# Block-causal attention with a ReGLU network: the last quarter of the result by row blocks on two queues, and another order of tiles 3 to 8

## The chip, the cores and the metric

The kernel runs on one core of a Trainium2 chip. The core has five engines, each of which carries out its own instructions in the order of the program: PE (matmuls; its weight loads, PEld, run beside the products), DVE (VectorE), ACT (ScalarE), POOL (GpSimd) and SP (SyncE, which here only issues transfers). An engine waits on semaphores for what another engine or a transfer has to deliver. The metric is the device time of one execution in microseconds; lower is better.

## The reference

```python
# 8 batches, 8 heads, 576 positions, head dim 64; blocks of 64 positions
scores = scale * np.matmul(q, k.transpose(0, 1, 3, 2))      # scale = 1/8
scores = np.where(block_i >= block_j, scores, -1e9)         # causal by blocks
attn = softmax(scores)
x = np.matmul(attn, v)  # -> [batch, position, head, dim] -> [4608, 512]
gate = np.maximum(x @ w_gate, 0.0)                          # w_gate [512, 1536]
val = x @ w_val                                             # w_val  [512, 1536]
out = (gate * val) @ w_out                                  # w_out [1536, 512]; out [4608, 512], fp32
```

## The kernel before

**Tiles.** The network is worked off in nine tiles of 512 rows. Tiles 0 to 7 are the first 512 positions of batches 0 to 7, and tile 8 is the last 64 positions of all eight batches. Attention runs ahead of the network: tiles 0 to 2 and the attention of batches 0 to 3 come in a hand-written order of their own (ORDER_0), and in each of tiles 3 to 6 the attention of the next batch, and the loads of the batch after that, are woven into the network's products. Tiles 7 and 8 have no attention beside them.

**The order.** Nothing is scheduled by a compiler: `program(j)` returns a function `do`, and a string of words (ORDER_3_6 for tiles 3 to 6, ORDER_7, ORDER_8) is read word by word; `w*n` repeats a word n times. Each word emits one step, and so the string sets the order of instructions on all engines at once. The words:

- `g8`, `v8`: a quarter (an atom) of a plain product with w_gate or w_val for 128 of the 1536 columns; four make one bank of 512 columns. `r8` is its relu on ACT, `h8` the multiply on DVE.
- `p37`: an atom of product 7 of pair 3. Pairs of column blocks (six pairs, 0 to 5) are done by a scheme of seven products in place of eight, so with sums of parts of x and of the weights as operands; each of the seven products has two atoms, each of two matmuls of 256 columns. `p3a`, `p3u`, `p3w` are ACT's copies of a bank to SBUF, `p3d`, `p3e`, `p3c` DVE's adds of a bank to such a copy, `p3r` a relu on ACT. `p3H` and `p3L` multiply gate by value into the two halves of hT, the low half always on DVE (line 1395), the high half on DVE or GpSimd (line 1391).
- `M1` to `M7`: an atom of one of the seven output products (line 1060), which read hT or sums of it. Six atoms make a whole product: three for the rows p = 0 and then three for p = 1.
- `oa`, `ou`, `ow`, `oy`: ACT copies a bank of the result to SBUF (line 1105); `od`, `oe`, `oc`: DVE adds a bank to such a copy (line 1099). The result has four quarters, c11, c12, c21 and c22; c12 is the bank `w` as it stands once M1, M6, M5 and M3 have been summed in it, c21 an earlier copy of `w` to which the bank of M7 and M4 is added.
- `S0` to `S2`: the store of a quarter by `put_block`; `P` is the store S3 of the tile before. In tiles 3 to 7 a store is one issue, by ACT (line 892). In tile 8 it is two issues (line 905), one for each half of the partitions, since its rows belong to eight batches; a table there gives the issuing engine by quarter.
- `X4` to `X7`, `Y4` to `Y7`: sums of parts of x (line 1161). `s1302`: part 3 of the sums of hT for the pairs 2 and 3 (line 1019). `U45`: a sum of weights, redone in each tile because its memory is shared.
- `A0` to `A3`: the score products of two heads of the next batch; `E0u`, `E0s` and so on the exps that follow on ACT (line 635); `C01` the zeroing of a corner of the exps; `V01` the products with v (line 778); `N01` the normalising on DVE.
- `l0` to `l10`, `w0` to `w5`: loads of q, k and of v in bf16 for the batch after next, issued by GpSimd (line 508). `d0` to `d3`: the transposes of q and k (qTm, kTm, qTt, kTt) by DMA, on SyncE's queue (line 518). `T0` to `T3`: the transposes of x into xT, also on SyncE's queue.

**Who does what.** The set ON_POOL names the steps that GpSimd does in place of DVE, with the tile ahead (`3X5`, `8s1202`). SLOTS, PAIR_BANK, OUT_BANK and AV_BANK name the buffer or PSUM bank of each step; there are two banks of a kind `sc`, one `one` and three `ffn`.

**The end of the program.** The last words of ORDER_8 are `M3*4 Sa M3*2 oy S0 oe S1`: the last product, a copy of all of c12 by ACT, its store, which the table gives to SyncE twice (`(0, 256)`), the add of c21 on DVE, and its store, which the table gives to ACT twice (`(1, 0)`). The words stand in each engine's program in this order, and each engine reaches its own as soon as what it needs is there.

Of the kernel before, what the change touches and what calls it, by code (L numbers as in the profile page):

```python
# [17 lines left out]
def kernel(  # L18
# [91 lines left out]
    ORDER_8 = """  # L110
        X4 p01 p17 p07 p21 p01 p07 p11*2 p17 p12 p21 p12 p0a p06 p1a p1c p06 p16*2 p0w
        p04*2 p0u p05 p0e p05 p0d p1u p15*2 p1w p14 p1d p14 p1e p1L p31*2 p02*2 p0c p03
        p2a p3a p03 p0r p0H p13*2 p1r p1H p26*2 p2u p27*2 p0L p41*2 p32*2 p3c p25 p36
        p2w p25 p36 p2d p24*2 p2e p4a p3u p37 p22*2 p2c p37 p23*2 p3w p2r p51*2 s0002
        p2L p35*2 p3d p42 P p5a p34*2 p3e p3L p42 p47*2 p4w p33*2 p56 p46 p3r s0202
        s0102 p4c p46 p4u p44 p52*2 p5c p56 p44 p4e p57*2 p2H p45*2 p4d p5u p55*2 p5w
        p5d M7 p54*2 p5e M1 p43 M1 p53*2 M2*2 p5r p4L p43 p4r p5L M1*4 oa p5H p4H s2002
        s2202 M2*4 p3H s1002 s1102 s2302 s2102 s1202 M6*5 M7 M6 ou s0302 ocb Sb oca M7*4
        M5*5 ow M4 M5 M4*3 od S2 M4*2 s1302 M3*4 Sa M3*2 oy S0 oe S1
# [40 lines left out]
        (7, 4): ('sc', 'ffn', 'one'),  # L160
        (7, 5): ('sc', 'ffn', 'ffn'),
        (8, 0): ('sc', 'one', 'one'),
        (8, 1): ('ffn', 'ffn', 'ffn'),
        (8, 2): ('sc', 'ffn', 'one'),
        (8, 3): ('ffn', 'ffn', 'one'),
        (8, 4): ('sc', 'sc', 'one'),
        (8, 5): ('ffn', 'ffn', 'ffn'),
# [1639 lines left out]
```

## Time and profile before

| | us |
|---|---|
| three runs | 346.49, 347.24, 347.37 |
| their median | 347.24 |
| the profiled execution's own time | 348.3 |
| its span, first to last instruction | 346.5 |
| busy in the span: PE / DVE / ACT / POOL | 333.9 / 239.8 / 211.2 / 202.4 |
| mean granted clock of PE | 0.998 |

The profile comes from one execution, with instruction times on each engine; the span is shorter than the execution's time by what lies ahead of the first and behind the last instruction. A row of the sums by stage gives a stretch of the span and the busy time of each engine in it. A row of the chain gives the start and length of a stretch of the work that ended last, its engine and line. A row of the waits reads: who waited, for which engine's line, the sum of the waits, their number, and the longest. An engine name with a q behind it (ACTq, SPq) is the engine's sequencer: there an issue of a transfer shows as the time that the engine was taken up with it.

### The profile page before, as it was taken

The numbers are of one execution on the slowest core, as the hardware profiler recorded it, in microseconds if no ns is written. First come the engines' busy times: TensorE is split into PE (matmuls) and PEld (weight loads), VectorE is DVE, ScalarE is ACT, GpSimd is POOL, SyncE is SP. The second block draws the span as 40 slices with busy tenths as digits, with TensorE's granted clock in tenths as the row PEclk, the third lists the DMA queues.
The fourth block names the chain that finished last, engine by engine and source line by source line (L and its number), as shares of the span: only waits on it lengthen the run. The fifth ranks groups of instructions, "written<-read, shape, count | busy, mean of one in ns | idle before, by whom it ended". The sixth has DMA issues, their size and how long they took to land.

```text
span 346.5 us, 8901 instructions
## 1 busy us (share of the span) xinstructions
PE 333.9 (96%) x3477; PEld 234.0 (68%) x3518; DVE 239.8 (69%) x561; ACT 211.2 (61%) x348; POOL 202.4 (58%) x249
## 2 busy tenths in 40 slices
PE   8999999999999999999999999999999999999993
PEld 4544455545545559676867787778777798878883
DVE  4854445768628887588638874788478877995991
ACT  4942757587325872787467865876487717626740
POOL 2766565588965902846866758675514673820720
PEclk9999999999999999999999999999999999999999
DMA  8999999999998994999399999999510030002004
GB/s 237 294 352 373 363 235 243 230 149 185 171 231 93 140 176 95 203 137 144 61 167 146 116 97 153 150 116 112 132 47 2 19 99 32 2 30 93 32 1 121
DMA packets 155402, 50.06 MB, mean 144 GB/s; under 512 B 134464, under 2 KB 151744, under 8 KB 155360
## 3 DMA queue, kind: packets, MB, share of 16 engines
q0 software_dynamic: 70528, 8.98, 44.5%
q1 hardware_dynamic: 77520, 32.52, 43.4%
q10 hardware_dynamic: 7312, 8.00, 8.0%
q8 instruction: 27, 0.44, 0.5%
q14 instruction: 15, 0.12, 0.1%
HBM read 37.75 MB, written 9.44 MB: 136 GB/s over the span
## 4 chain that ended last, share of the span: by engine, by line
PE 84%; ACT 4%; DVE 3%; DMA 3%; ACTq 2%; issue 2%; SPq 0%; POOL 0%; DVEq 0%
PE ffnp L1169 15%; PE ffnp L1353 10%; PE sc L1353 8%; PE one L1060 7%; PE ffnp L1329 6%; PE ffnp L1060 6%; PE ffnp L1272 6%; PE one L1353 5%; PE sc L1060 4%; PE sc L630 3%; PE ffnp L778 2%; PE one L630 2%; DMA stage<-in_moe_w_val_dram 2%; ACTq L892 2%; PE sc L778 2%
## 5 line engine op out<-in xcount | busy, mean ns | idle before, releaser
L635 ACT ACTIVATE attnT<-sc 128x1024 bf16<-128x1024 f32 x56 | 56.2, 1035 | 0.0
L1179 ACT ACTIVATE gate_sb<-ffnp 128x512 bf16<-128x512 f32 x35 | 20.5, 598 | 27.2 <-PE ffnp L1169 24.3
L1169 PE MATMUL ffnp<-xT,wg 128*128 128x512 bf16 x130 | 36.2, 379 | 0.6
L1060 PEld LDWEIGHTS <-stage 128*128 128x128 bf16 x336 | 31.9, 98 | 4.5 <-DVE stage L1019 0.5
L1353 PEld LDWEIGHTS <-stage 128*128 128x128 bf16 x288 | 27.6, 98 | 7.6 <-issue 0.7
L778 PEld LDWEIGHTS <-attnT 128*128 128x128 bf16 x640 | 26.8, 98 | 8.2 <-DVE xnat L717 1.2
L1169 PE MATMUL ffnp<-xT,wv 128*128 128x512 bf16 x108 | 31.3, 380 | 0.2
L1189 DVE TENSOR_TENSOR hT<-gate_sb,ffnp 128x512 bf16<-128x512 bf16 x28 | 19.2, 684 | 14.3 <-PE ffnp L1169 11.5
L1353 PEld LDWEIGHTS <-wg 128*128 128x128 bf16 x224 | 21.5, 98 | 7.9 <-issue 3.0
L1060 PEld LDWEIGHTS <-hT 128*128 128x128 bf16 x252 | 23.7, 98 | 4.0 <-DVE hT L1395 1.3
L1379 DVE TENSOR_TENSOR ob<-ffnp,ob 128x512 f32<-128x512 f32 x29 | 19.9, 688 | 8.9 <-ACT ob L1375 6.6
L508 POOL DMA_DIRECT2D v_bf<-in_v_dram x30 | 24.5, 838 | 2.7 <-PE ffnp L1169 1.1
L1353 PEld LDWEIGHTS <-wv 128*128 128x128 bf16 x224 | 21.4, 98 | 5.1
L1272 PE MATMUL ffnp<-wo,hT 128*128 128x512 bf16 x91 | 23.1, 379 | 0.2
L1169 PEld LDWEIGHTS <-wg 128*128 128x128 bf16 x144 | 13.4, 98 | 13.8 <-issue 0.5
L1169 PEld LDWEIGHTS <-wv 128*128 128x128 bf16 x144 | 13.0, 98 | 14.3 <-issue 1.5
L508 POOL DMA_DIRECT2D q_bf<-in_q_dram x20 | 18.1, 910 | 6.3 <-DVE recip L751 6.2
L1324 ACT ACTIVATE gate_sb<-ffnp 128x512 bf16<-128x512 f32 x29 | 17.8, 612 | 6.4 <-PE ffnp L1353 4.8
L642 ACT ACTIVATE attnT<-one 128x512 bf16<-128x512 f32 (+1 forms) x28 | 15.2, 543 | 10.5 <-PE ffnp L630 10.4
L1391 POOL TENSOR_TENSOR hT<-gate_sb,q_bf 128x512 bf16<-128x512 bf16 x8 | 10.2, 1285 | 19.4 <-ACT gate_sb L1324 19.3
L1105 ACT COPY ob<-one 128x512 f32<-128x512 f32 x13 | 7.6, 586 | 22.0 <-PE one L1060 22.0
L630 PEld LDWEIGHTS <-kTm 64*128 64x128 bf16 x384 | 11.4, 94 | 13.1 <-issue 7.0
(223 smaller groups left out, 919.3 us busy)
## 6 DMA issues: line engine op xcount, KB each, us to landing
out_dram<-ob ACTq DMA_DIRECT2D x28, 256.0 KB, 3.2
stage<-in_moe_w_val_dram SPq DMA_DIRECT2D x6, 512.0 KB, 8.7
stage<-in_moe_w_gate_dram SPq DMA_DIRECT2D x6, 512.0 KB, 8.3
stage<-in_moe_w_out_dram SPq DMA_DIRECT2D x6, 512.0 KB, 10.5
q_bf<-in_q_dram POOLq DMA_DIRECT2D x20, 128.0 KB, 5.4
k_bf<-in_k_dram POOLq DMA_DIRECT2D x20, 128.0 KB, 5.7
v_bf<-in_v_dram POOLq DMA_DIRECT2D x20, 128.0 KB, 6.7
stage<-in_v_dram SPq DMA_DIRECT2D x19, 128.0 KB, 5.4
```

Source lines behind the costliest of these rows:

```text
L508: ins = nc.gpsimd.dma_start(dst, part_of)
L630: nc.tensor.matmul(o, kTm[b % 2][head_of(hh), c, hp, :], qT, start=True, stop=True)
L635: return lambda: nc.scalar.activation(at[:, :, lo : lo + 512], sc, AF.Exp, scale=scale)
L778: nc.tensor.matmul(av[:, p, :], at[:, col : col + 128], v_bf[b % 2][:, c, h, :], start=(p == 0), stop=(c == p), skip_group_check=True,)
L1060: nc.tensor.matmul(to, sums.of(c)[which][:, 128 * p : 128 * p + 128], right, start=first, stop=(c == 5), skip_group_check=True,)
L1169: nc.tensor.matmul(to, (wg, wv)[t][f // 4][:, c, 128 * (f % 4) : 128 * (f % 4) + 128], x[:, c], start=(c == 0), stop=(c == 3),)
L1179: nc.scalar.activation(gate_sb, gate, AF.Relu)
L1189: nc.vector.tensor_tensor(out=h, in0=gate_sb, in1=val, op=AX.mult)
L1272: nc.tensor.matmul(op, hT[f][:, 128 * s : 128 * (s + 1)], wo[f // 4][:, f % 4, n0:n1], start=(f == 0), stop=(f == 11),)
L1329: nc.tensor.matmul(to, (wg, wv)[t][f // 4][:, c, 128 * (f % 4) : 128 * (f % 4) + 128], x[:, c], start=(c == 0), stop=(c == 3),)
L1353: nc.tensor.matmul(st[key][:, 256 * k : 256 * k + 256], left[:, c, 128 * k : 128 * k + 128], right[:, c], start=new and (k, c) == (0, 0), ...
L1379: nc.vector.tensor_tensor(out=t, in0=st[n, of], in1=t, op=AX.add)
```

## The change

The last quarter of tile 8's result, c12, is no longer copied by ACT in one piece and stored by SyncE in two issues. The new steps `oya` and `oyb` copy the rows p = 0 (ACT, behind the third atom of M3) and the rows p = 1 (DVE, behind the sixth), and `Sya` and `Syb` store each with two issues of half the size, one by SyncE and one by ACT. The store of c21 goes from ACT and ACT to GpSimd and SyncE.

Beside this the strings for tiles 3 to 8 are replaced by others with the same products, copies, adds and stores. What differs most: the transposes `d0` to `d3` stand earlier than `T0`, with `d1` to `d3` ahead of all of `T0` to `T3`; S2 is stored behind `od` instead of at the end of the tile; the numbers of M2 and M3 behind M4 change; and the order of pairs in tiles 7 and 8 is another. ON_POOL changes: in tiles 3 to 6 the multiply 5H goes from GpSimd to DVE, X4, X5 and X7 are on GpSimd in place of X5 and X6, the sums of hT there are s0002, s1002, s1102 and s2302 in place of five others, and of the corners C01, C10, C20, C21, C30, C31 in place of C01, C11, C20, C21, C31. U03 is on GpSimd and U46 is not. In tile 8 seven sums of hT are on GpSimd in place of three. SLOTS, PAIR_BANK, OUT_BANK and AV_BANK follow the new order and are left out below.

```diff
--- before.py
+++ after.py
...
@@ -83,40 +83,40 @@
         x15 f*2 U57 f*20
     """.split()
     ORDER_3_6 = """
-        X5 A0 E0u E0s E0f g0*2 p12 g1 p12 g1 l0 X7 X6 X4 l1 l2 l3 p11*2 p1a g0*2 C00 p1c
-        E0t r0 g1 p17*2 p16 g1 K k p16 C01 V00 N00 v1*2 p1u p15*2 p1w p1d V01 N01 p14*2
-        p1e p1L v1 p13*2 v0*2 A1 P v1 r1 h1 p1r v0 p21 E1t E1u v0 h0 E1s p21 p2a p22*2
-        p2c p31 E1f p27 g8*2 p27 p2w p26*2 p2u U45 p1H s0002 p37 p31 p3a C10 p24*2 p2e
-        p32 p25*2 p2d l4 l5 l6 w0 l7 l8 s0202 C11 p2L w1 g8 p36*2 p3u V11 N11 p37 p3w g8
-        r8 p35*2 p3d p23*2 p2r p34*2 p3e p32 p33*2 p3r p3c A2 E2t p51*2 v8*2 p57*2 E2u
-        p52*2 p2H l9 l10 s0102 p3L p5a w2 w3 p3H s1002 p5c v8 p56 v8 h8 p56 p5w E2s C21
-        p54*2 U05 p5u p5e g9 E2f g9*3 r9 V10 N10 p55*2 p5d p5L v9*2 A3 E3t E3u v9*2 h9
-        d0 d1 T0 T1 d2 p53*2 p5r C20 U46 V20 M1 p5H s1102 N20 s2102 s2002 s1202 s2202
-        E3f V21 M1*3 M7*2 M1*2 E3s C30 M7*2 C31 N21 d3 T2 w4 s1302 s2302 U07 w5 oa M7*2
-        ow M6*2 V30 N30 M6*4 V31 N31 T3 M4*2 ou M5*6 U06 od M4*4 oe S1 M2 U03 s0302 M3*6
-        oy S0 U47 U43 M2*5 S2 oc
+        A0 l0 X5 w0 g1*3 E0t X7 X6 E0s g0*4 E0u C01 E0f C00 p11 K p11 p12 p1a p12 p1c l1
+        k g1 r1 p17*2 w1 p16*2 p1u V00 N00 v1*2 p15*2 p1w p1d P r0 X4 l2 l3 d0 V01 N01
+        v1 p14*2 p13*2 p1r p1e v0*2 v1 A1 E1t E1s v0*2 p1H h1 h0 p1L p21*2 p2a p22*2 p2c
+        p27*2 p2w p26 U05 p26 p2u U06 l4 l5 l6 p31*2 p3a p24*2 p2e w2 s0002 p25*2 p2d
+        U45 g8 E1f E1u C11 g8*2 p36*2 p2L p37 p3u p37 p3w w3 C10 V11 p23 N11 p23 p2r
+        p35*2 p3d g8 r8 p34*2 p3e p32*2 p3c s0102 p33*2 U46 l7 l8 l9 p3L d1 l10 d2 d3 w4
+        w5 p3r p3H A2 E2u E2t p51*2 p5a p2H s1002 E2s C21 v8*2 p52*2 s1102 p5c p57 v8
+        p57 p5w v8 h8 p56*2 p5u V10 N10 T1 T0 g9 p54*2 p5e g9*3 p55*2 p5d E2f r9 U43 A3
+        E3u v9*2 p53*2 v9 s1202 C20 M1*2 p5L M1*2 M7 v9 s0202 U07 s0302 M1*2 V21 M7 E3f
+        p5r E3s p5H C30 h9 s2002 s2102 s2202 E3t C31 V20 s2302 V31 oa M6*4 V30 M6*2 N21
+        N20 T2 M7*4 ou N30 N31 M5*3 M2 M5*3 ow od S2 U03 M4*3 T3 M2 M4 s1302 U47 M3 M4*2
+        oe S1 M2 M3*5 oy S0 M2*3 oc
     """
     ORDER_7 = """
-        X5 p11*2 p1a p01*2 p0a X7 X6 p21 p02 p12*2 p1c X4 p07*2 p16 p02 p06 p0c p16 p06
-        p0w p04*2 p21 p22 p0u p0e p1u p05*2 p0d p22 p15 p17 p0L p2a p2c p17 p15 p1w p1d
-        p03*2 p26 p0r p0H p31*2 p14 p27 p3a p27 p14 p1e p13 p37 p13 p1r p1H s0002 p1L
-        s0102 p36 p26 p36 p32*2 p3c Y5 p51*2 p37 p2u p25 p2w p25 p2d p24*2 p2e p5a p56
-        p3u p35*2 p23 p41 p23 p41 p3w p3d p2r p2H p34*2 p57 p33*2 p57 p56 p2L p4a p46
-        p3e p3L p52*2 p3r p5u p5w p42 p5c p42 p4c p3H p55*2 p5d p46 p47 p54 p47 p4u p54
-        p5e p4w p45*2 p4d M2 p44*2 p4e p53*2 M1*2 p5L p4L p5r p43 M2 p43 p4r p5H s0202
-        p4H s2002 M1*2 M7 s1002 s1202 M1*2 M2*3 s2202 s1102 M7 M2 oa M6*6 s2102 M7*4 P
-        ou M5*6 s2302 Y7 s0302 s1302 ow od S2 M4*5 oc M4 oe M3*6 oy S1 S0 Y6
+        p11*2 p12 p01*2 p21 p02 p12 Y5 X5 X7 X6 X4 p1a p1c p0a p02 p0c p07 p06*2 p0u p07
+        p0w p16 p17 p16 P p1u p05 p17 p05 p0d p04*2 p0e p21 p15*2 p1w p2a p03 p22 p03
+        p14*2 p0r p0H p1d p13*2 p1r p22 p26*2 p31 p2u p0L p2c p1e p1H p31 p3a p37*2
+        p27*2 p2w p1L s0002 s0202 p25 p32 p25 p2d p36*2 p3u p24*2 p2e p32 p3w p23*2 p2r
+        p2H p51 p3c p35*2 p3d p34*2 p3e p51 p5a p41*2 p4a p33*2 p3r p3H p56*2 p5u s1002
+        p2L p46 p52*2 p57*2 p5w p46 p4u p3L s1102 p5c s0102 p55*2 p5d p47 p42*2 p4c p47
+        p54 p4w p54 p5e p45*2 p4d p44*2 p4e p5L p4L M1 M2 p53 p43 M1 p53 p5r p5H M7*2
+        p43 M2 p4r p4H s2002 s2202 s2102 s1202 M1*4 M2*4 oa M6*6 ou s1302 M7*4 M5*6 ow
+        od S2 M4*6 s0302 M3 s2302 Y7 M3*5 oe S1 oy S0 Y6 oc
     """
     ORDER_8 = """
-        X4 p01 p17 p07 p21 p01 p07 p11*2 p17 p12 p21 p12 p0a p06 p1a p1c p06 p16*2 p0w
-        p04*2 p0u p05 p0e p05 p0d p1u p15*2 p1w p14 p1d p14 p1e p1L p31*2 p02*2 p0c p03
-        p2a p3a p03 p0r p0H p13*2 p1r p1H p26*2 p2u p27*2 p0L p41*2 p32*2 p3c p25 p36
-        p2w p25 p36 p2d p24*2 p2e p4a p3u p37 p22*2 p2c p37 p23*2 p3w p2r p51*2 s0002
-        p2L p35*2 p3d p42 P p5a p34*2 p3e p3L p42 p47*2 p4w p33*2 p56 p46 p3r s0202
-        s0102 p4c p46 p4u p44 p52*2 p5c p56 p44 p4e p57*2 p2H p45*2 p4d p5u p55*2 p5w
-        p5d M7 p54*2 p5e M1 p43 M1 p53*2 M2*2 p5r p4L p43 p4r p5L M1*4 oa p5H p4H s2002
-        s2202 M2*4 p3H s1002 s1102 s2302 s2102 s1202 M6*5 M7 M6 ou s0302 ocb Sb oca M7*4
-        M5*5 ow M4 M5 M4*3 od S2 M4*2 s1302 M3*4 Sa M3*2 oy S0 oe S1
+        p07 X4 p07 p01*2 p0a p17 p11*2 p12 p1a p12 p1c p06*2 p31 p0w p0u p16*2 p1u p04*2
+        p0e p17 p1w p05*2 p0d p15*2 p1d p14*2 p1e p1L p31 p3a p03*2 p0r p37 p13*2 p1r
+        p1H p21 p0H s0002 p21 p02*2 p0c p0L s0102 p36 p27*2 p2a p26*2 p32 p37 p32 p3c
+        p41*2 p2u p25*2 p36 P p2w p2d p24*2 p3w p2e p4a p34*2 p3u p3e p23*2 p2r p2H
+        p22*2 p2c p35*2 p3d p51 p47 p51 p5a p42 p47 p4w p46 p52 p42 p3L p46 p4c p2L p44
+        p33*2 p4u p44 p4e p3r p45*2 p4d s0202 p4L p52 p56*2 p5c M2 p57*2 p5u p55 p43 p55
+        p5w p5d M2 p43 p4r p54*2 p5e p5L p4H M1 p53 M7 p53 p5r M1*4 M2 p3H M1 M2*3 p5H
+        s2002 s1102 M7 s1002 s1202 s2202 s2302 s1302 s2102 oa oca M6 s0302 M6*5 ou Sa
+        M7*4 M5*6 ow od S2 ocb Sb M4*4 M3*3 oya Sya M4*2 oe S1 M3*3 oyb Syb
     """
     ONLY = {
         'U03': (6,),
...
     ON_POOL = set(
         """
-        32H 35H 3C01 3C11 3C20 3C21 3C31 3X5 3X6 3s0202 3s0302 3s1002 3s1302
-        3s2302 42H 45H 4C01 4C11 4C20 4C21 4C31 4X5 4X6 4s0202 4s0302 4s1002
-        4s1302 4s2302 52H 55H 5C01 5C11 5C20 5C21 5C31 5X5 5X6 5s0202 5s0302
-        5s1002 5s1302 5s2302 62H 65H 6C01 6C11 6C20 6C21 6C31 6X5 6X6 6s0202
-        6s0302 6s1002 6s1302 6s2302 70H 71H 72H 73H 7X4 7X5 7s0002 7s0102 7s0302
-        7s1002 7s1102 7s2302 80H 81H 82H 83H 8s0102 8s1002 8s1202 U05 U06 U43
-        U45 U46
+        32H 3C01 3C10 3C20 3C21 3C30 3C31 3X4 3X5 3X7 3s0002 3s1002 3s1102
+        3s2302 42H 4C01 4C10 4C20 4C21 4C30 4C31 4X4 4X5 4X7 4s0002 4s1002
+        4s1102 4s2302 52H 5C01 5C10 5C20 5C21 5C30 5C31 5X4 5X5 5X7 5s0002
+        5s1002 5s1102 5s2302 62H 6C01 6C10 6C20 6C21 6C30 6C31 6X4 6X5 6X7
+        6s0002 6s1002 6s1102 6s2302 70H 71H 72H 73H 7X4 7X5 7X7 7Y6 7s0002
+        7s0202 7s1002 7s1102 7s1202 7s2302 81H 82H 83H 8s0002 8s0102 8s0202
+        8s1002 8s1102 8s1302 8s2302 U03 U05 U06 U43 U45
         """.split()
     )
...
@@ -898,8 +898,8 @@
             for i in range(2):
                 b0 = 4 * hi + 2 * p0 + i
                 eng = {
-                    (0, 256): (nc.sync, nc.sync),
-                    (1, 0): (nc.scalar, nc.scalar),
+                    (0, 256): (nc.sync, nc.scalar),
+                    (1, 0): (nc.gpsimd, nc.sync),
                     (1, 256): (nc.sync, nc.gpsimd),
                 }.get((hi, n0), (nc.scalar, nc.sync))
                 eng[i].dma_start(
@@ -1109,6 +1109,15 @@
                 add(st["c21"], st["v"])
             elif name == "oc":
                 add(st["c11"], st["x"])
+            elif name in ("oya", "oyb"):
+                if "c12" not in st:
+                    st["c12"] = ob()
+                p = "ab".index(name[2])
+                copy = (nc.scalar.copy, nc.vector.tensor_copy)[p]
+                copy(half(st["c12"], p), half(st["w"], p))
+            elif name in ("Sya", "Syb"):
+                p = "ab".index(name[2])
+                put_block(j, 0, 256, half(st["c12"], p), p, p + 1)
             elif name in ("oca", "ocb"):
                 p = "ab".index(name[2])
                 add(half(st["c11"], p), st["x", p])
...
```

More of the change, by code (lines that the diff above doesn't have):

```diff
@@ L45 @@
         "sc": (
-            "010101010101010010101010101010101010101010101010101010101001100100110101"
-            "10011001001101011001100100110101100110010011010110001010101"
+            "010101010101010010101010101010101010101010101010101010101001011100111010"
+            "01101000110001011001011100111010011010001100010110010110101100"
         ),
@@ L50 @@
             "021021021020210210210210210210120210120202010101210120201201120120210211"
-            "201021102101020120120120121201202101202101202101210201021201021001001201"
-            "201020121020120020021021020102120102100100120120102012102012002002102100"
-            "0201210210021210102"
+            "201021102101020120120120121201202101202101202101210221012021210220201212"
+            "012201021202012212102021022101202121022020121201220102120201221210202100"
+            "20012120102202210"
         ),
         "ob": (
-            "043210432104314013240312402312301243021340231230124302134023123012430213"
-            "402312302130214201240312"
+            "043210432104314024130413023413240213241320341304201304130234132402132413"
+            "203413042310423402431024"
         ),
         "gate_sb": (
-            "021021021021021021021021021021021021021201012010212102120101201021210210"
-            "21021021"
+            "021021021021021021021021021021021021021102210122011202110221012201120210"
+            "21021201"
         ),
@@ L155 @@
         (6, 5): ('ffn', 'one', 'ffn'),
-        (7, 0): ('ffn', 'one', 'sc'),
-        (7, 1): ('sc', 'sc', 'ffn'),
+        (7, 0): ('ffn', 'one', 'ffn'),
+        (7, 1): ('sc', 'sc', 'sc'),
         (7, 2): ('ffn', 'ffn', 'ffn'),
         (7, 3): ('one', 'ffn', 'sc'),
[L160 to L167, printed above, removed]
+        (7, 4): ('ffn', 'ffn', 'one'),
+        (7, 5): ('sc', 'ffn', 'sc'),
+        (8, 0): ('one', 'sc', 'sc'),
+        (8, 1): ('ffn', 'sc', 'ffn'),
+        (8, 2): ('sc', 'one', 'ffn'),
+        (8, 3): ('ffn', 'ffn', 'ffn'),
+        (8, 4): ('sc', 'one', 'ffn'),
+        (8, 5): ('ffn', 'one', 'sc'),
     }
@@ L188 @@
     }
-    AV_BANK = {0: ('ffn', 'one'), 1: ('sc', 'sc'), 2: ('ffn', 'ffn'), 3: ('ffn', 'sc')}
+    AV_BANK = {0: ('one', 'ffn'), 1: ('sc', 'sc'), 2: ('sc', 'ffn'), 3: ('one', 'ffn')}
     LAST_CHUNKS = {}
```

2 lines of the change are left out of this document (1 added, 1 removed).

## The prediction

> **What bounds the kernel now.** I read the page's head first, then the sums by stage, the chain that ended last, the waits of TensorE, and last the order of time around three places: the starts of tiles, the start of each tile's output products, and the tail.
>
> ```profile
> span 346.5 us, 8901 instructions
> ...
> PE 333.9 (96%) x3477; PEld 234.0 (68%) x3518; DVE 239.8 (69%) x561; ACT 211.2 (61%) x348; POOL 202.4 (58%) x249
> ```
>
> ```profile
> 175.30:212.00 36.70, 35.65 (x412) 27.44 (x416) 25.74 (x61) 24.73 (x41) 25.56 (x32) 1.00 1.26 128
> 212.00:248.00 36.00, 35.57 (x412) 27.45 (x416) 25.75 (x61) 24.80 (x41) 24.77 (x31) 1.00 1.45 132
> ...
> 284.00:312.80 28.80, 27.92 (x254) 24.43 (x252) 25.39 (x42) 14.75 (x27) 13.47 (x11) 1.00 0.11 38
> 312.80:341.30 28.50, 28.20 (x252) 24.11 (x250) 22.28 (x40) 15.23 (x28) 9.26 (x8) 1.00 0.13 38
> 341.30:346.50 5.20, 0.00 (x0) 0.00 (x0) 0.00 (x0) 0.59 (x1) 0.00 (x0) 0.85 0.60 152
> ```
>
> The rows are tiles 4, 5, 7, 8 and the tail; after the length come the busy times of PE, PEld, DVE, ACT and POOL, the granted clock (1.00 wherever products run) and the DMA's share. PE is the bound: in tile 5 it is busy 35.57 of 36.00 us. The change removes no product, so it can win only what PE stands idle in tiles 3 to 8, and part of the last row, 5.20 us in which PE does nothing.
>
> ```profile
> 175.35 1.25 ACTq L892
> ...
> 283.92 1.81 ACTq L892
> ...
> 303.02 1.21 DVE hT L1395 x2
> ...
> 310.17 1.31 PE sc L1060 x12
> ...
> 315.41 0.57 PE sc L1353 x4
> ```
>
> ```profile
> PE ffnp L1060 <- DVE hT L1395: 0.8, 2, 0.5
> ...
> PEld L1060 <- DVE hT L1395: 1.3, 2, 0.8
> PEld L1353 <- issue: 0.5, 1, 0.5
> ```
>
> The chain is PE almost everywhere; the rows above are where it leaves PE or where PE is slow. The waits are those of tiles 7 and 8 alone. The third M1 of a tile needs the low halves of pair 4 and pair 5, and both tiles wait for that (L1395, by the weight loads: 1.3 us in two waits, the longest 0.8, so 0.8 and 0.5). At the start of tiles 4 and 7 ACT is held by a store that takes 1.25 and 1.81 us to issue. A product of 256 columns takes 0.109 us (1.31 by 12), an atom of two 0.218 us.
>
> **The tail.** Before, all of the last quarter (the program's c12) is copied by ACT after the last product (0.59 us), and then SyncE issues both stores, one after the other.
>
> ```profile
> 341.31 0.59 ACT L1105 COPY ob<-ffnp 128x512 f32<-128x512 f32 x1 [3.29 <-PE ffnp L1060]
> 341.93 1.25 SPq L905 DMA_DIRECT2D out_dram<-ob  x2
> ```
>
> ```profile
> out_dram<-ob SPq DMA_DIRECT2D x3, 128.0 KB, 2.7
> out_dram<-ob SPq DMA_DIRECT2D x2, 64.0 KB, 2.2
> out_dram<-ob ACTq DMA_DIRECT2D x2, 64.0 KB, 2.3
> out_dram<-ob POOLq DMA_DIRECT2D x1, 128.0 KB, 2.6
> ```
>
> ```profile
> L1099 DVE TENSOR_TENSOR ob<-ffnp,ob x3: 415/419/693, 336.4 to 338.9; 128x256 f32<-128x256 f32 x2, 128x512 f32<-128x512 f32 x1
> ```
>
> The second store is issued at 342.6 (341.93 and half of 1.25), lands 2.7 later at 345.3, and 1.2 us pass from there to the end. After, only rows p = 1 remain behind the last product. VectorE first finishes oe, an add of 512 columns, 0.69 us (the row's longest; in ns: least, median, most): the three last atoms of M3 (0.65 us) run beside it, so it ends at about 341.35. oyb follows, 0.42 us by the half add (a half copy isn't in the trace), and ends at 341.75. SyncE issues its half of S1 at 341.35 and its half of Syb at 341.95, 0.6 us each; ACT issues the other half of Syb at 341.75. Landings: 341.95 + 2.2 = 344.15, 341.75 + 2.3 = 344.05, SyncE's S1 341.35 + 2.7 = 344.05, GpSimd's S1 341.35 + 2.6 = 343.95. The last falls 1.15 us earlier than before. The bounds: a gain of 0.65 us if a store of 64 KB among these takes the 2.7 of a big one, and 0.35 us if it takes 3.0. I take 1.0, nearer to the two rows of 64 KB, with something off as four stores land at once. oya and Sya (0.4 us of copy, two issues) lie beside two atoms of M4 and three of M3, 1.1 us; if PE had to wait for oya, because it reads the bank that the second half of M3 writes, the two atoms of M4 (0.44 us) cover it.
>
> The Trainium skill, page "DMA: Bandwidth & Descriptors", section "Issuing engines are not separate DMA queues", says that issuing from several engines saves only the time of the issue itself. By that rule alone the tail gains one issue, 0.6 us, and the sum below would be 0.4 us smaller; the 0.5 us between the rows of 128 and 64 KB is the size's, which the rule leaves out.
>
> **The start of the output products (tiles 7 and 8).** Tile 7: between the last atom of pair 4's fourth product and the third M1 stood seven atoms (p53 twice, M1 twice, p43 twice, M2 once), 1.53 us; after the change ten, 2.18 us. VectorE has the same adds and multiplies to do in that time. The wait of 0.7 us shrinks by 0.65; I take 0.5 (bounds 0 and 0.7). Tile 8: behind p55 before, p54 must end (three atoms), then p5e, p4L and p5L on VectorE, and PE has eleven atoms, 2.4 us; after, p4L is done earlier but p54 ends after four atoms, and PE has nine, 1.96 us. VectorE's end: 0.87 (four atoms) + 0.7 (p5e, an add) + 0.6 (p5L, 1.21 by two) + some 0.2 of hand-over = 2.4 us, so the wait stays at 0.4 us: taken as 0, bounds a gain of 0.4 and a loss of 0.4.
>
> **The starts of tiles 4, 7 and 8.**
>
> ```profile
> 211.64 0.90 ACTq L892 DMA_DIRECT2D out_dram<-ob  x2
> ...
> 312.89 1.76 ACTq L892 DMA_DIRECT2D out_dram<-ob  x2
> ```
>
> ```profile
> q8 instruction: 1, 0.02, 3.8%
> ```
>
> Behind the copy oy ACT issued S0 and S2, then the first exps or copies of the next tile. At tile 5 the two issues took 0.90 us, at tile 8 1.76, and at tiles 4 and 7 the second alone took the 1.25 and 1.81 above. The queue's row is of 283.9 to 285.8: one packet of the instruction queue moved there, as in the windows of the two other slow starts, and none at tile 5. A fetch of instructions seems to hold an issue until it is over. PE lost 0.7 us at tile 4 (36.70 against 36.00), 0.5 us at tile 7 (the wait put down to an issue) and about 0.4 us at tile 8 (0.57 for four products in place of 0.44, and a little at each of the next groups). The change sends S2 earlier, so one issue is left there; but fewer M2 stand behind M3 (three in tiles 3 to 6, none in tile 7), so S0 is issued 0.3 to 1.0 us after the next tile's start, inside the same fetch. Tile 4: nothing changes. Tile 7 needs p0a after ten atoms, 2.2 us: no wait with a free issue (0.4 + 0.5 + 0.6), 0.7 us with a held one. Tile 8 needs p0a after nine atoms, 2.0 us: none, or 0.5 us. Half of the first, as its issue lies at the fetch's edge, and most of the second, 0.4: 0.75 us against 0.9 before, a gain of 0.15, taken as 0.2; bounds a gain of 1.6 (none is held, tile 4's 0.7 goes too) and a loss of 0.3.
>
> **Inside tiles 3 to 6.** The multiply 5H (0.6 us, the row of L1395) goes from GpSimd to VectorE, X4 and X7 for X6 and other sums change places one for one; I count 0.5 us more for VectorE a tile, beside 25.75 of 36.00. The waits of PE there are a few tenths a tile. Reading the new order queue by queue I find the same number of narrow places (p16 behind p1a, p27 behind the second exp, p25 behind p2u), each 0.1 us, and late exps of the fourth pair of heads (E3s and E3t just ahead of V20 and V31). I take a loss of 0.4 us for the four tiles, bounds 0 and 1.5.
>
> **The sum.** -1.0 - 0.5 + 0 - 0.2 + 0.4 = -1.3 us against the profiled execution's own 348.3 us (its span 346.5 and 1.8 around it). The median of the runs, 347.24, is 1.1 below that execution; the difference applied to it gives 345.9, and I say 346.0. A difference of 0.3%, 1.04 us, is about the least that a measurement of this kernel tells from none.
>
> **Rivals.** First, slower, by SyncE's queue. Before, the transposes of x (T0 and T1) stand behind kTm alone; after, behind kTm, qTt and kTt, all of which wait for loads that GpSimd issues later (l7 to l10 after C10).
>
> ```profile
> 219.28 4.50 SPq L518 DMA_TRANSPOSE qTm<-q_bf  x1
> 219.84 1.79 POOL L508 DMA_DIRECT2D k_bf<-in_k_dram  x2
> 230.90 3.04 SPq L518 DMA_TRANSPOSE kTm<-k_bf  x1
> ```
>
> ```profile
> xT<-xnat SPq DMA_TRANSPOSE x24, 4.1
> ```
>
> In tile 5 the k loads issued beside qTm's transpose let kTm begin only 11 us later. After, by the same rows, l8 is issued about 15 us into the tile, kTm begins at 24 to 25, SyncE is free of kTm, qTt and kTt at 30, and T3, the fourth xT behind them, is issued at 33.5 to 34.5 and lands up to 4.1 later, 36 to 38.5; the next tile starts at 36.0 (tile 5's length) and first needs that part of x some 2.2 us later, with the fourth g0. For it: the DMA's share is over 1 in these tiles. Against: x is used later than before (there p12, after 1.3 us). It decides from a landing at 38.2 on: at 1 us beyond, three tile starts (4, 5, 6) lose 1 us each, -1.3 + 3 = +1.7, 348.9 us.
>
> Second, no change, by GpSimd's sums in tile 8.
>
> ```profile
> 306.96 2.57 POOL L1019 TENSOR_TENSOR stage<-hT,stage 128x512 bf16<-128x512 bf16 x2 [4.35 <-DVE stage L1019]
> 307.14 1.38 DVE L1161 TENSOR_TENSOR perm<-xTt 128x512 bf16<-128x512 bf16 x1
> ```
>
> ```profile
> L1019 DVE TENSOR_TENSOR stage<-hT x32: 406/420/540, 109.6 to 335.7; 128x512 bf16<-128x512 bf16 x32
> ```
>
> A VectorE sum, 0.42 us by the median of the last row, took 1.38 beside a GpSimd sum. The new tile 8 puts s2302 and s1302 on GpSimd just as VectorE does s2102 and s0302: s2102 can be 0.95 us late for the third M7, which has about 0.4 us to spare. With that 0.55 us, both issues held (0.3) and 0.4 inside tiles 3 to 6, -1.5 becomes -0.25: 347.0. The Trainium skill, page "SBUF — State Buffer", section "Who interferes with whom", has it that a VectorE instruction with two SBUF inputs and a GpSimd instruction that reads SBUF exclude each other for a whole instruction. Our row agrees, 1.38 for 0.42; by the rule each such meeting of the new order costs one GpSimd sum at most.
>
> Third, every wait goes: -1.0 - 0.7 - 0.4 - 1.6 = -3.7, 343.5 us. Against it: the fetches are there in three of the starts, and the order alone doesn't take them away.
>
> **How the numbers follow.** The forecast (345 to 346.6) 0.42, of it 0.07 above 346.2; no change 0.23; slower 0.27; every wait gone 0.08. So faster 0.35 + 0.08 = 0.43, same 0.07 + 0.23 = 0.30, slower 0.27. The range leaves out the last case and the upper part of the slower one: 344.3 to 348.9; the forecast's own is 345.0 to 346.6.
>
> **What would show it.** Right: PE's last product to the span's end falls from 5.2 to about 4.2 us, with SyncE's last store issued by 0.6 us after the copy; the waits of PE on L1395 fall below 1.0 us in all; tile 5 stays within 35.6 to 36.4 us. Wrong: a wait of PE on xT at the starts of tiles 4 to 6, VectorE sums of over 1 us beside GpSimd's in tile 8, or stores of 64 KB that take 3 us.

## The result and the profile after

The changed kernel took 345.31 us (344.99 to 345.60) against 347.0 us (346.49 to 347.37) before: a ratio of 0.9939, interval 0.9921 to 0.9957. It is 1.7 us faster. The profiled execution took 344.99 us. Its page begins:

```profile
span 343.2 us, 8912 instructions
## 1 busy us (share of the span) xinstructions
PE 332.7 (97%) x3477; PEld 233.7 (68%) x3518; DVE 239.9 (70%) x557; ACT 210.4 (61%) x348; POOL 207.0 (60%) x255
```

PE is still the bound, and the spans differ by 3.3 us, twice what the medians do; more on this below. The sums by stage, for tiles 3 to 8 and the tail, each from its first product to the first product of the next one (columns as in the prediction):

```profile
139.00:174.75 35.75, 35.49 (x412) 27.41 (x417) 25.75 (x60) 24.96 (x42) 23.67 (x30) 1.00 1.29 139
174.75:210.41 35.66, 35.38 (x414) 27.34 (x418) 27.07 (x61) 24.51 (x42) 26.20 (x32) 1.00 1.26 131
210.41:246.05 35.64, 35.38 (x412) 27.41 (x417) 26.63 (x61) 24.50 (x42) 23.07 (x29) 1.00 1.27 131
246.05:281.60 35.55, 35.28 (x412) 27.52 (x417) 26.76 (x64) 24.40 (x42) 17.28 (x19) 1.00 0.18 47
281.60:309.63 28.03, 27.77 (x254) 24.43 (x252) 23.57 (x39) 15.19 (x28) 14.49 (x12) 1.00 0.11 37
309.63:338.11 28.48, 28.09 (x253) 24.36 (x251) 22.47 (x38) 15.83 (x29) 13.72 (x11) 1.00 0.13 37
338.11:343.22 5.11, 0.28 (x3) 0.00 (x0) 0.59 (x2) 0.00 (x0) 0.62 (x1) 0.73 0.57 163
```

The same cuts (in us) of the kernel before and of every kernel that was run. The tail here begins with the last product's start and not, as in the prediction, with its end:

| kernel | tile 3 | 4 | 5 | 6 | 7 | 8 | tail |
|---|---|---|---|---|---|---|---|
| before | 35.95 | 36.72 | 35.99 | 35.78 | 28.85 | 28.38 | 5.51 |
| before_again | 35.94 | 36.44 | 35.99 | 35.77 | 28.89 | 28.54 | 5.51 |
| after | 35.75 | 35.66 | 35.64 | 35.55 | 28.03 | 28.48 | 5.11 |
| s2_early | 35.94 | 35.87 | 35.87 | 35.71 | 28.30 | 28.53 | 5.49 |
| n36 | 35.75 | 36.05 | 35.65 | 35.54 | 28.31 | 28.49 | 5.50 |
| n78 | 35.95 | 36.48 | 36.00 | 35.77 | 28.02 | 28.48 | 4.91 |
| old_tail | 35.75 | 35.85 | 35.65 | 35.55 | 28.03 | 28.30 | 5.78 |
| no_s1 | 35.75 | 35.84 | 35.65 | 35.55 | 28.02 | 28.48 | 4.44 |
| tail_q | 35.90 | 35.65 | 35.65 | 35.55 | 28.03 | 28.48 | 4.93 |
| old_pool | 37.92 | 37.82 | 37.82 | 38.47 | 28.02 | 28.49 | 4.93 |
| s2_late | 36.00 | 36.19 | 36.18 | 36.08 | 33.20 | 28.47 | 4.97 |
| new_pool | 38.46 | 39.36 | 39.46 | 37.85 | 28.53 | 28.95 | 5.51 |
| h5_pool | 36.00 | 35.64 | 35.65 | 35.55 | 28.02 | 28.48 | 4.94 |
| t8_dve | 35.76 | 35.64 | 35.64 | 35.55 | 28.03 | 28.73 | 4.96 |

Between the two profiled executions, tiles 3 to 6 became 0.20, 1.06, 0.35 and 0.23 us shorter, tile 7 0.82; tile 8 is 0.10 longer, the tail 0.40 shorter; 0.34 lies ahead of tile 3, where the program is the same. The starts of tiles 4 and 7 in ACT's timeline after:

```profile
174.20 0.58 ACT L1105 COPY ob<-ffnp 128x512 f32<-128x512 f32 x1 [4.00 <-PE ffnp L1060]
174.81 0.38 ACTq L892 DMA_DIRECT2D out_dram<-ob  x1
175.24 0.60 ACT L642 ACTIVATE attnT<-one 128x512 bf16<-128x512 f32 x1 [0.46 <-PE one L630]
...
281.76 0.38 ACTq L892 DMA_DIRECT2D out_dram<-ob  x1
282.24 0.59 ACT L1384 COPY ob<-sc 128x512 f32<-128x512 f32 x1 [0.51 <-PE sc L1362]
```

Where two issues stood, of which the second took 1.25 and 1.81 us, there is one of 0.38, and the next tile's first exp or copy follows at once. The third M1 (lines of after are a few higher: L1404 is the old L1395), by the waits of the weight loads of tiles 7 and 8, went from 0.8 and 0.5 us to 0.5 and 0.6, or from 1.3 to 1.2 in all:

```profile
PEld L1060 <- DVE hT L1404: 1.2, 2, 0.6
```

The tail, from the timelines of ACT and VectorE, and the transfers issued between 338.4 and 340 (KB each, us to landing):

```profile
337.15 0.37 ACT L1117 COPY ob<-ffnp 128x256 f32<-128x256 f32 x1 [2.39 <-PE ffnp L1060]
```

```profile
337.58 0.69 DVE L1099 TENSOR_TENSOR ob<-sc,ob 128x512 f32<-128x512 f32 x1 [1.01 <-PE sc L1060]
338.49 0.43 DVE L1117 COPY ob<-ffnp 128x256 f32<-128x256 f32 x1 [0.22 <-PE ffnp L1060]
```

```profile
out_dram<-ob SPq DMA_DIRECT2D x1, 128.0 KB, 3.3
out_dram<-ob POOLq DMA_DIRECT2D x1, 128.0 KB, 2.8
out_dram<-ob ACTq DMA_DIRECT2D x1, 64.0 KB, 3.0
out_dram<-ob SPq DMA_DIRECT2D x1, 64.0 KB, 2.9
```

The copy oyb takes 0.43 and starts as forecast. The two last stores of 64 KB, issued at 338.95 (ACT) and 339.17 (SyncE), take 3.0 and 2.9 us, not 2.2 and 2.3.

### The profile page after: what moved, and what is told of

Its sections match the earlier page's. It is cut to its first block, busy times and chain, and to the rows that moved or that the text cites. A ratio compares the mean times of both kernels' runs of the same rounds, so it can differ in the third digit from the quotient of the medians.

```text
span 343.2 us, 8912 instructions
## 1 busy us (share of the span) xinstructions
PE 332.7 (97%) x3477; PEld 233.7 (68%) x3518; DVE 239.9 (70%) x557; ACT 210.4 (61%) x348; POOL 207.0 (60%) x255
## 4 chain that ended last, share of the span: by engine, by line
PE 85%; POOL 4%; issue 3%; DVE 3%; ACT 2%; DMA 1%; POOLq 0%; DVEq 0%
PE ffnp L1178 16%; PE ffnp L1060 10%; PE ffnp L1362 10%; PE sc L1362 7%; PE ffnp L1338 7%; PE ffnp L1281 6%; PE one L1362 5%; PE sc L1060 4%; PE sc L630 3%; PE one L630 2%; PE ffnp L778 2%; POOL stage L1019 2%; PE one L1178 2%; PE one L778 2%; PE sc L778 1%
## 5 line engine op out<-in xcount | busy, mean ns | idle before, releaser
L635 ACT ACTIVATE attnT<-sc 128x1024 bf16<-128x1024 f32 x56 | 57.3, 1037 | 0.0
L1105 ACT COPY ob<-ffnp 128x512 f32<-128x512 f32 x19 | 11.1, 585 | 38.8 <-PE ffnp L1060 38.8
L1019 POOL TENSOR_TENSOR stage<-hT 128x512 bf16<-128x512 bf16 x19 | 23.4, 1239 | 7.9 <-DVE hT L1434 3.0
L1060 PEld LDWEIGHTS <-hT 128*128 128x128 bf16 x252 | 24.5, 98 | 4.9 <-DVE hT L1404 1.2
L1518 POOL MEMSET attnT<- 64x256 bf16 x26 | 7.9, 306 | 30.2 <-ACT attnT L635 19.6
L1388 DVE TENSOR_TENSOR ob<-ffnp,ob 128x512 f32<-128x512 f32 x30 | 20.6, 688 | 5.0 <-ACT ob L1384 2.9
L1170 POOL TENSOR_TENSOR perm<-xT 128x512 bf16<-128x512 bf16 x10 | 12.1, 1214 | 17.2 <-DMA xT<-xnat 17.2
```

The lines of the kernel that those rows point to most:

```text
L635: return lambda: nc.scalar.activation(at[:, :, lo : lo + 512], sc, AF.Exp, scale=scale)
L1019: (eng or nc.vector).tensor_tensor(out=of(part), in0=a, in1=b, op=op)
L1060: nc.tensor.matmul(to, sums.of(c)[which][:, 128 * p : 128 * p + 128], right, start=first, stop=(c == 5), skip_group_check=True,)
L1388: nc.vector.tensor_tensor(out=t, in0=st[n, of], in1=t, op=AX.add)
```

## The experiments

**before_again**: the kernel before, unchanged.

> The kernel before, unchanged, to see what one execution differs from another. The profiled execution of before took 348.3 us where the median of its runs is 347.0, so 1.3 us of the 3.3 us between the two spans may belong to that one execution. If the slow start of tile 4 (36.72 us against 36.00 in tile 5, with a store's issue of 1.25 us) comes from where the program's instructions lie, it is there again: tile 4 36.5 to 36.9, tiles 3, 5 and 6 within 0.1 of 35.95, 36.00 and 35.78. If it is chance, tile 4 falls to about 36.0 or another tile start is slow.

It took 347.9 us; this kernel, no_s1, new_pool, h5_pool and t8_dve were timed once, and what is read from them is the trace. The slow starts of tiles 4 and 7 are there again (36.44 and 28.89; tile 4 in n78 below too, 36.48), so they belong to this program and not to one execution. ACT's timeline at tile 4:

```profile
174.62 1.40 ACTq L892 DMA_DIRECT2D out_dram<-ob  x2
176.07 0.60 ACT L642 ACTIVATE attnT<-ffnp 128x512 bf16<-128x512 f32 x1 [1.48 <-PE sc L630]
```

Over the 29 runs of before beside the first four kernels, its time went from 346.16 to 348.37 (median 347.22). Both profiled executions of before, 348.3 and 347.9, are from the upper part. This is why the traces differ by more than the medians: 1.1 to 1.3 us of the 3.3 are this execution's, and another 0.3 come from the profiled execution of after, which lies below its median.

**s2_early**: one word of ORDER_3_6 in the kernel before.

```diff
-  ... ou M5*6 U06 od M4*4 oe S1 M2 U03 s0302 M3*6 oy S0 U47 U43 M2*5 S2 oc
+  ... ou M5*6 U06 od S2 M4*4 oe S1 M2 U03 s0302 M3*6 oy S0 U47 U43 M2*5 oc
```

> Before, with one word moved: in tiles 3 to 6 the store S2 stands behind od, as after the change, and not at the tile's end. Theory A, the end of the prediction's part on starts: at tile 4's start ACT is held because the second issue falls into a fetch of instructions; with one issue less there, the exps start on time and tile 4 takes 36.0 in place of 36.7 us; tiles 3, 5 and 6 are as before within 0.1; the time falls by 0.5 to 0.8. Theory B: ACT is held by whatever else goes on there (GpSimd issues four loads beside it), and the single S0 is held as well: tile 4 stays at 36.5 to 36.8, the time the same within 0.3.

346.73 us, ratio 0.9985 (0.9971 to 0.9998). Tiles 4 and 7 by stage:

```profile
174.75:210.62 35.87, 35.50 (x412) 27.45 (x417) 25.73 (x61) 24.81 (x41) 25.55 (x33) 1.00 1.31 129
...
282.20:310.50 28.30, 27.75 (x254) 24.46 (x252) 25.23 (x42) 14.84 (x27) 13.49 (x11) 1.00 0.09 29
```

Theory A: tile 4 became 0.6 to 0.85 us shorter and tile 7 0.55 to 0.6, and tiles 5 and 6, where nothing was held, 0.12 and 0.07: even an unheld second issue (0.48 us at 212.06 before) delays the exps of the next tile, the first one by 0.1 us. That the lone S0 was free is what the prediction had not reckoned with; it is issued inside a fetch here (by the packet records of the instruction queue 174.15 to 175.30, the issue 174.38 to 174.76) and still takes 0.38.

**n36** and **n78**: the kernel before with the new strings, engines, banks and slots of tiles 3 to 6 alone, and of tiles 7, 8 and the tail alone (the slots renamed at the seam).

> Before, with the new order, engines and banks of tiles 3 to 6 alone; tiles 7 and 8 and the tail as before. Theory A, from the trace after (tiles 3 to 6 took 35.75, 35.66, 35.64 and 35.55 us, before 35.95, 36.72, 36.00 and 35.78): these tiles carry most of the gain, 1.85 us of the span, of which 1.06 at tile 4, and the time falls by 1.0 to 1.9. Theory B, as I predicted (a loss of 0.4 inside these tiles): what the two traces differ by is the slow execution that was profiled; the time is within 0.5 of before.

> Before, with the new order of tiles 7 and 8 and the new tail, tiles 3 to 6 as before. From the trace after: tile 7 28.0 (before 28.85), tile 8 28.5 (28.4), from the last product's start to the end 5.1 (5.5): the time falls by about 1.1, and with the run of tiles 3 to 6 alone it adds up to the whole change. If the two parts don't add up, something crosses from tile 6 into tile 7 (the place of the fetches of instructions at its start).

n36: 346.02 us, 0.9958 (0.9942 to 0.9974). n78: 346.43 us, 0.9981 (0.9966 to 0.9996). 0.42% and 0.19% add up to the whole change's 0.61% (each known to some 0.15%). Theory A holds for n36; n78 gained 0.7 to 0.8 us, not the 1.1 that were expected. n36's tile 5, with none of its issues held, is 0.35 us shorter than before and 0.22 shorter than s2_early's, so that much a tile is the order's beyond S2 (its tile 4, 36.05, has one held issue, of 0.78 us):

```profile
211.02:246.67 35.65, 35.38 (x413) 27.43 (x418) 26.87 (x61) 24.50 (x42) 24.14 (x30) 1.00 1.22 129
246.67:282.21 35.54, 35.28 (x412) 27.52 (x417) 26.75 (x64) 24.40 (x42) 15.92 (x18) 1.00 0.18 47
282.21:310.52 28.31, 27.77 (x254) 24.45 (x252) 25.23 (x42) 14.97 (x28) 13.48 (x11) 1.00 0.11 37
```

Tile 7 of n36, in its old order, has 28.31, as in s2_early: there S2's place in tile 6 is worth 0.55 of tile 7's 0.82 us. But tile 7's new order is worth all of it by itself (28.02 in n78, where S0 and S2 still stand at the end of tile 6), so the two shares overlap. ACT's row of n78 at that start shows why:

```profile
282.81 0.90 ACTq L864 DMA_DIRECT2D out_dram<-ob  x2
```

The two issues take 0.90 us together and none is held. By the packet records the fetch of instructions begins 1.1 us into tile 7 here, where in before it began 0.4 us into it.

**old_tail**: after, with the tail of before.

```diff
-        M7*4 M5*6 ow od S2 ocb Sb M4*4 M3*3 oya Sya M4*2 oe S1 M3*3 oyb Syb
+        M7*4 M5*6 ow od S2 ocb Sb M4*4 M3*3 M4*2 M3*3 oy S0 oe S1
-                    (0, 256): (nc.sync, nc.scalar),
-                    (1, 0): (nc.gpsimd, nc.sync),
+                    (0, 256): (nc.sync, nc.sync),
+                    (1, 0): (nc.scalar, nc.scalar),
```

> After, with the old tail alone: the last words of tile 8 are M4*4 M3*3 M4*2 M3*3 oy S0 oe S1, c12 is copied whole by ACT and stored by SyncE twice, c21 by ACT twice. Theory A, from the two traces: the tail is worth 0.4 us, from the last product's start to the end 5.5 in place of 5.1, and PE's wait of 0.19 us for the copy oya goes: in all 0.2 slower than after. Theory B, the prediction's term: the tail is worth 1.0 and only this execution had slow stores; then old_tail is 0.8 slower than after.

345.43 us, 0.9952 (0.9939 to 0.9964). By the trace the tail is 0.67 longer and tile 8 0.18 shorter, so 0.5 in all: midway between the theories. Of the 0.67, 0.27 lie behind the last store's landing (1.37 us to the end of the span, in after 1.10); why is not known. The 0.18 is PE's wait for the copy oya, which the prediction had as covered.

```profile
309.93:338.23 28.30, 27.94 (x254) 24.35 (x251) 22.27 (x38) 15.46 (x28) 13.70 (x11) 1.00 0.12 36
338.23:344.01 5.78, 0.27 (x3) 0.00 (x0) 0.34 (x1) 0.58 (x1) 0.00 (x0) 0.96 0.58 148
```

**no_s1**: after, without the word S1 in ORDER_8, so that this kernel leaves out the store of c21 of tile 8.

> After, without the store S1 of tile 8: the quarter c21 of the last 64 positions is never stored. In after the last stores of 64 KB took 2.9 to 3.0 us to land where before 2.2 to 2.3 was seen for that size. Theory A, contention: they share the DMA engines with S1's 256 KB, issued 0.1 to 0.7 us ahead of them; without S1 they land in 2.2 to 2.4 and, as SyncE is free for its half at once, the last product's start to the end takes 4.2 us. Theory B, these stores take 2.9 us at the end of the program whatever goes beside them: 4.9 us, the SyncE issue alone being 0.2 earlier.

344.93 us. The last two stores:

```profile
out_dram<-ob SPq DMA_DIRECT2D x1, 64.0 KB, 2.2
out_dram<-ob ACTq DMA_DIRECT2D x1, 64.0 KB, 2.4
```

The tail is 4.44. Theory A: these stores are slow because S1's 256 KB go at the same time. 256 KB beside a store need not do it, though: in before, a store of 64 KB at 340.34, 0.4 and 0.7 us behind two stores of 128 KB, took 2.4; in the tail the stores of the copy oya and the other half of oyb's go as well. In its sentence on issuing engines the prediction cited the Trainium skill ("DMA: Bandwidth & Descriptors", "Issuing engines are not separate DMA queues"): DMAs of all engines share the same DMA engines, and several issuers save only the issue. By that rule alone the tail was to gain 0.6 us. The 0.4 to 0.6 measured agree in size, and no_s1 shows the sharing: 0.6 to 0.7 us on each store against after.

**tail_q**: after, with `(1, 0): (nc.gpsimd, nc.scalar)`.

> After, with one entry of the table changed: the second half of S1 is issued by ACT and not by SyncE, which is then free when the copy oyb is done. SyncE's last issue was at 339.17, 0.22 us behind ACT's at 338.95. If the last landing follows the last issue, the end comes 0.2 us earlier (4.9 from the last product's start) and the time is 0.2 below that of after, which is less than can be measured; if the stores share what carries them, the end stays at 5.0 to 5.1.

344.83 us (344.55 to 344.98), 0.9930 (0.9918 to 0.9942) of before: the fastest of all, though from after, at 0.9939, it can't be told apart. The tail is 4.93, but the five other kernels with the tail of after had 4.91 to 4.97, so the 0.2 us that were expected are not shown: the 5.11 of after was a long one. This fits the second theory, that what carries the stores is shared, but it doesn't decide: the last issue came only 0.1 us earlier than in n78 (0.95 us behind the last product's start, not 1.03). old_tail, timed beside it, was 0.6 slower.

**old_pool** and **new_pool**: the new order with GpSimd's old steps in tiles 3 to 6, and the old order with the new steps.

```diff
old_pool:  - 3X4 3X5 3X7 3C01 3C10 3C20 3C21 3C30 3C31 3s0002 3s1002 3s1102 3s2302 U03
           + 35H 3X5 3X6 3C01 3C11 3C20 3C21 3C31 3s0202 3s0302 3s1002 3s1302 3s2302 U46   (4, 5, 6 alike)
new_pool:  the reverse, in the kernel before
```

> After, but in tiles 3 to 6 GpSimd has the steps that it had before (5H, X5, X6, the five old sums, C01 C11 C20 C21 C31, U46 and not U03); order and banks are new. After, these tiles took 35.75, 35.66, 35.64 and 35.55 us. Theory A, the assignment carries the gain (the new order was laid out for when GpSimd's sums hold VectorE's): each tile is 0.3 us or more longer, 36.0 and above, and the time rises by 1 to 2. Theory B, the order carries it (the first atoms of pair 1 and the exps no longer meet at the tile's start): the tiles stay within 0.15 of after and the time within 0.6.

> Before, with GpSimd's steps in tiles 3 to 6 as after the change; order and banks of before. The run with the new order and the old steps took 37.8 to 38.5 us a tile. Theory A, order and assignment only fit each other: this one too is slower, tiles 3, 5 and 6 by 0.5 us or more each, with PE waiting for GpSimd's sums of x or zeroed corners. Theory B, the new assignment is better by itself (GpSimd works while it is free): tiles 3, 5 and 6 within 0.2 of before or shorter.

old_pool: 354.41 us, 1.0209 (1.0191 to 1.0226). new_pool: 359.28 us. Theory A in both (the new steps are no gain by themselves), and with more than was expected: 2.2 to 2.9 us a tile in the one, 2.1 to 3.5 in the other. PE's waits in tile 5, first of old_pool, then of new_pool:

```profile
PE sc L750 <- DVE attnT L1487: 0.7, 1, 0.7
PE sc L1334 <- DVE perm L1142: 0.5, 1, 0.5
PE ffnp L1310 <- DVE ob L1360: 0.2, 1, 0.2
```

```profile
PE ffnp L749 <- POOL attnT L1489: 1.0, 1, 1.0
PE one L1031 <- DVE stage L990: 0.9, 1, 0.9
PE sc L749 <- DVE attnT L1486: 0.5, 1, 0.5
PE one L1333 <- ACT ob L1355: 0.4, 1, 0.4
```

PE waits for zeroed corners (attnT), sums of x (perm) and sums of hT (stage); these rows make 1.4 of the 2.2 us in old_pool's tile 5 and 2.8 of the 3.5 in new_pool's, the rest lies in shorter waits. On the engine that the order was not written for the step stands behind something: in old_pool a corner behind VectorE's adds and multiplies, in new_pool one behind three loads that GpSimd issues.

```profile
229.33 0.68 DVE L1376 SCALAR_TENSOR_TENSOR hT<-ob,ob 128x512 bf16<-128x512 f32 x1
230.09 0.17 DVE L1487 MEMSET attnT<- 64x128 uint32 x1
```

```profile
219.91 2.66 POOL L479 DMA_DIRECT2D q_bf<-in_q_dram  x3
222.61 0.31 POOL L1489 MEMSET attnT<- 64x256 bf16 x1
```

**s2_late**: after, with S2 at the end of tiles 3 to 6 again (`od U03 ... oy S0 M2*3 S2 oc`).

> After, with one word moved back: in tiles 3 to 6 the store S2 stands at the tile's end again, behind S0, as before the change. Theory A, from the runs so far: two issues back to back are what costs; the second is held until a fetch of instructions is over (it ended 0.39 to 0.40 us behind the fetch in each of the nine cases seen on ACT), and the exps of the next tile stand behind it. Tile 4 and tile 7 become 0.4 to 0.8 us longer, 5 and 6 up to 0.1; the time rises by 0.5 to 1.0. Theory B, the new order has more products ahead of the first one that needs an exp's bank (seven atoms of g where there were two of g and some of pair 1), so that a late exp is covered: every tile within 0.15 of after, the time within 0.3.

351.67 us, 1.0099 (1.0074 to 1.0125): neither theory. Tiles 4 to 6 are 0.5 us longer although no issue was held in them; A's mechanism is there (two issues, then the exps, 0.3 us of PE at the first atom of pair 1 and 0.2 at a later one), but tile 7 grew by 5.2 us. Its waits, and four stretches of tile 7 by stage:

```profile
ACT ob L1356 <- DMA out_dram<-ob: 3.4, 1, 3.4
PE ffnp L1334 <- ACT ob L1356: 3.4, 1, 3.4
```

```profile
285.70:289.23 3.53, 0.17 (x3) 0.00 (x1) 0.55 (x2) 0.58 (x1) 0.67 (x1) 1.00 0.14 47
289.23:290.18 0.95, 0.95 (x9) 0.86 (x9) 0.67 (x1) 0.32 (x1) 0.00 (x0) 1.00 0.00 0
290.18:293.60 3.42, 3.42 (x18) 2.43 (x17) 1.05 (x2) 1.92 (x4) 0.00 (x0) 0.50 0.23 79
293.60:296.00 2.40, 2.40 (x24) 2.14 (x22) 1.67 (x4) 1.51 (x3) 0.53 (x1) 1.00 0.00 0
```

A copy of pair 0 goes into one of the five output buffers, and in the new rotation that buffer is the one that S2 empties. The store, issued at 284.09, lands at 288.51, the copy starts at 288.59, PE stands still for 3.4 us, and 0.95 us after it has resumed it runs at a granted clock of 0.50 for 3.4 us (18 products; at 1.00, 24 go in the 2.4 us behind them). Of the 5.2 us, 3.4 are the wait and the rest the clock.

**h5_pool**: after, with 5H of tiles 3 to 6 on GpSimd.

> After, with the one multiply 5H of tiles 3 to 6 on GpSimd again. The prediction had its move to VectorE as a cost of 0.5 us of VectorE and 0.1 us a tile. Theory A, the move is a gain: on GpSimd it takes 1.2 us in place of 0.65, and the corner C30, s2302 and C31 queue behind it, so that the third atom of M6 or M7 and the product V30 come late: tiles 3 to 6 are 0.3 us or more longer each. Theory B, the prediction's: the tiles are the same or up to 0.1 shorter.

345.05 us. Theory B: tiles 4 to 6 are as after within 0.02 (tile 3 has 36.00, as in s2_late, where the others with this order and these engines have 35.75 to 35.90; what makes the difference is not known). In tiles 4 to 6 the multiply costs nothing on either engine.

```profile
210.64:246.29 35.65, 35.65 (x417) 27.39 (x418) 26.54 (x60) 24.50 (x42) 25.32 (x31) 1.00 1.19 127
```

**t8_dve**: after, without `8s1302` and `8s2302` in ON_POOL.

> After, with the sums s2302 and s1302 of tile 8 on VectorE. They were the second rival's mechanism: on GpSimd they hold VectorE's sums (one of 1.05 us was seen there, where 0.42 is usual). Theory A, that meeting costs PE nothing, as the sum that it holds (s0302) is needed only by M3; on VectorE they stand ahead of s2102, which the third atom of M7 needs, and tile 8 becomes 0.1 to 0.4 us longer than its 28.48. Theory B, the rival: PE waits for what GpSimd holds, and tile 8 becomes shorter by 0.2 or more.

345.09 us; tile 8 is 0.25 longer. Theory A: PE stands still for 0.24 us ahead of the third atom of M7, at 333.1. The sum that GpSimd held in after (the row below) was s0302, which only M3 reads, over 2 us later.

```profile
309.62:338.35 28.73, 28.26 (x253) 24.21 (x251) 22.57 (x40) 15.83 (x29) 11.14 (x9) 1.00 0.13 37
```

```profile
332.74 1.05 DVE L1019 TENSOR_TENSOR stage<-hT,stage 128x512 bf16<-128x512 bf16 x1
```

## Why the prediction was right, and where its steps were wrong

The time, 346.0 forecast and 345.31 measured, is within the range and on the forecast side, but that is in part luck: the sum of -1.3 came to about the right size by terms that were not. Of the signs that were named for right, two came (the last issue 0.25 us behind the copy, tile 5 at 35.64) and two did not (4.2 us behind the last product, waits on hT below 1.0); of those for wrong, two of three came (a sum of 1.05 us on VectorE, stores of 64 KB of 3 us). Against the spans (-3.3):

| step of the prediction | forecast | measured |
|---|---|---|
| the tail | -1.0 | -0.4 (-0.5 to -0.6 elsewhere) |
| third M1, tile 7 | -0.5 | -0.3 |
| tile 8 behind its start | 0 | +0.5 |
| starts of tiles 4, 7, 8 | -0.2 | about -1.6 |
| inside tiles 3 to 6 | +0.4 | about -1.1 |
| ahead of tile 3, the same program | 0 | -0.3 |

**The tail.** The steps were right (oyb 0.43 us, issues 0.25 us behind the copy at the latest), the size was not: the store of 64 KB was taken as 2.2 to 2.3 us from four rows: three had only other stores of 64 KB beside them (2.05 to 2.29 us), the fourth took 2.41 beside 256 KB. In the tail S1 and the stores of oya go beside it, and it took 2.9 to 3.0; the bound of 0.35 us for 3.0 was the one that came true. The span behind the last product's end fell from 5.2 to 4.8, not to 4.2.

**The start of the output products.** Tile 7's wait shrank by 0.3 and not 0.5; tile 8's stayed (0.5 to 0.6), as forecast. By the weight loads the sum of the two is 1.2 us, and not below the 1.0 that was named as the sign. What was missed in tile 8 are three new waits of PE by the starts of its products: 0.18 at 326.4 (pair 2), 0.14 at 336.1 (the first atom of M3 waits until od has read its bank) and 0.19 at 337.3 (oya, said to be covered by two atoms of M4). They ate the 0.4 us that tile 8's start gave back.

**The starts of tiles.** This step failed in its mechanism. It took each issue inside a fetch as held, and the fetches as staying where they were, so that moving S2 left S0 held half the time. In eleven traces a store's issue by ACT that began inside a fetch near tile 4's start, with none close before it, passed in 0.38 to 0.39 us. 14 issues were held, twelve of them close behind another one, and all ended 0.38 to 0.41 us behind the fetch, which is the length of a free issue. It isn't a law: in n36 and no_s1 an S0 over 0.8 us behind the issue before it took 0.78 and 0.57. And at tiles 7 and 8 S0 met no fetch at all: in after it is issued 0.2 and 0.8 us into them, and the fetches begin 1.3 and 1.8 us into them, in before 0.4 and 0.6. Why they came later is open. The Trainium skill ("Runtime: NRT & Kernel Launch", "Instruction fetch mechanics") calls the cost of such a block of 16 KiB mostly hidden. For PE, whose instructions these most likely are, by their number (27 blocks for some 7,000 products and weight loads), the traces agree (in tile 5 of after three blocks came, and PE stood idle for at most 0.26 of 35.64 us); for the issue of a transfer on ACT or SyncE they do not (on SyncE, 0.95 us at 140.67 in after, until 0.39 behind the fetch).

**Inside tiles 3 to 6.** The forecast had the wrong sign. The 0.28 us that PE lost 1.8 us into tiles 5 and 6, at the first atom of pair 1, was among the "few tenths" and taken as staying. It is the end of a chain of ACT: copy, two issues, two exps, then the bank. S2's place takes off one link, but that alone left 0.22 us of it (s2_early), as the first exp then waits for its scores; the new order has seven atoms of g there, and the wait is gone. The 5H term (0.1 a tile) is 0, by h5_pool.

**The rivals.** The transposes behind d1 to d3 did not come late: kTm was issued 20.8 us into tile 4 (24 to 25 forecast), T3 at 31.4, landing at 33.8, and x was first needed at about 38. GpSimd's sums in tile 8 held one of VectorE's, 1.05 us, and no product; by the rule that the prediction cited beside this rival a meeting costs the one that waits at most one sum, which 1.05 for 0.42 bears out. "Every wait goes" (343.5) came nearest for the starts.

**What stays open.** S2's place is worth 1.3 us in the traces (before_again against s2_early, tiles 4 to 7) but 0.5 in the medians. The two executions lie differently: before_again is 0.7 us above the median of before, s2_early's traced one 0.4 below its own. There is no trace of before near its median, so how often its starts are held was not seen; n78, 0.1 from its median and with the old tiles 3 to 6, has the slow start of tile 4. Nor was it settled what decides whether an issue inside a fetch is held, or what moves a fetch.
